# Soft-capped attention and MLP: the 64 left-over keys of two head pairs scored together, with longer tanh and exp and another order of transfers

## The chip, the cores and the metric

The kernel runs on one core of a Trainium2 chip. The metric is device time in microseconds of one execution; the time before is the median of three runs. All rows below come from one profiled execution of the kernel before.

## The reference

Attention with a tanh cap on the scores over 4 batches and 12 heads of 448 tokens and 64 dimensions, and behind it an MLP of 768 to 2048 to 768 with a squared ReLU on the 1792 tokens.

```python
scores = scale * np.matmul(q, k.transpose(0, 1, 3, 2))
scores = cap * np.tanh(scores / cap)
attn = np.exp(scores - np.max(scores, axis=-1, keepdims=True))
attn = attn / (np.sum(attn, axis=-1, keepdims=True) + 1e-09)
attn_out = np.matmul(attn, v)
x = attn_out.transpose(0, 2, 1, 3).reshape(B * S, H * D)
h = np.maximum(x @ w_in, 0.0)
out = h * h @ w_out
```

## The kernel before

Heads are taken two at a time: a "group" n is one pair of heads, 24 groups in all, and one round of the loop at line 498 works on group n and finishes group n - 1. One head of the pair lies in partitions 0 to 63 ("top"), the other in 64 to 127 ("bottom"). Scores are held with keys in the partitions and the 448 queries in the columns. The 448 keys of a head are three tiles of 128 (u = 1, 2, 3) and a rest of 64 (u = 0). A full tile of both heads fills two PSUM banks (128 x 896 on ScalarE); the rest of 64 keys of both heads fills one bank (128 x 448), the one head in its top half, the other in its bottom half.

The order on TensorE, ScalarE, VectorE, GpSimd and SyncE is the order in which the code is written (a manual schedule). A round does, with the names that the rows use:

- TensorE: `scores` of u = 1, 2, 3, then of u = 0 (`sc`); for group n - 1 `pv_half` (the 64 rest keys times v into `pa`, and times ones into `pb`), `sums` (`pb<-add,ones`) and `pv` (`pa<-p,vn`). Three score tiles of two banks each rotate, and one `pa` and one `pb`.
- ScalarE: tanh of u = 1 and 2, exp of both together (128 x 1792), tanh of u = 3 and u = 0, exp of both together (128 x 1344), and `evac`, the copy of `pa` of group n - 1 to SBUF (`e<-pa`). There are two `e` tiles, so the copy of group n - 1 needs the tile that `normalise` of group n - 3 reads.
- VectorE: `add_p3` of group n - 1 (`add<-add,p`), `turn_kq` of group n + 1 (a 32 x 32 transpose that makes q and k usable, `kq<-kqn`), `invert` of group n - 2 (`cmp`), a step of decoding MLP weights, `add_p` of group n (needs the first exp), `take_sums` (copy of `pb`, `es<-pb`), `normalise` of group n - 3 (`x<-e,rb` and two more), another decoding step. Some decoding steps (Abs, L44) are on ScalarE.
- SyncE issues the transfers, in this order: `spread` of group n - 3 (two transfers that read the inverted sums from DRAM into all partitions, `rb<-rd`), four loads of q for group n + 3, `rd<-cmp` of group n - 2 (inverted sums to DRAM) and `cmp<-es` of group n - 1 (two transfers). A transfer waits on the queue until what it reads is there, and what stands behind it waits too. `rb<-rd` waits for `rd<-cmp` of the round before to have landed.

So a group's row sums go from `es` through `cmp`, `rd` and `rb` back to VectorE, over two rounds. After the loop TensorE goes on with the first matrix product of the MLP; `unit(0, 0)` of it already stands in the last round, ahead of `pv_half` of the last group.

Of the kernel before, what the change touches and what calls it, by code (L numbers as in the profile page):

```python
# [10 lines left out]
F32 = mybir.dt.float32  # L11
# [4 lines left out]
ACTF = mybir.ActivationFunctionType  # L16
# [172 lines left out]
def tile_softcap_attention_mlp(ctx, tc, q, k, v, cap, w_in, w_out, out):  # L189
    nc = tc.nc  # L190
    B, H, S, D = q.shape
    NT, DM = out.shape
    DFF = w_in.shape[1]
    P = 128
# [8 lines left out]
    scale = 1.0 / float(D) ** 0.5  # L203
# [4 lines left out]
    NKV = 3  # L208
# [24 lines left out]
    qks = const.tile([P, 1], F32, name="qks")  # L233
# [4 lines left out]
    pp = actx.enter_context(tc.tile_pool(name="p", bufs=2))  # L238
    ep = actx.enter_context(tc.tile_pool(name="ep", bufs=2))
    ps_s = actx.enter_context(tc.tile_pool(name="ps_s", bufs=3, space=PSUM))  # L240
# [7 lines left out]
    vn = [keep.tile([P, NS, D], F32, name=f"vn{i}") for i in range(NKV)]  # L248

    ones = keep.tile([P, D], F32, name="ones")  # L250
# [63 lines left out]
    top, bottom = slice(0, D), slice(D, P)  # L314

    def load_kq(n, i, *queues):
        b, j = divmod(n, NPAIR)
        for a in range(4):
            h, w = divmod(a, 2)
            x = (k, q)[i][b, 2 * j + h, :, 32 * w:32 * w + 32].rearrange("(t r) e -> r t e", r=32)  # L320
            queues[a % len(queues)].dma_start(out=kqn[n % NKQ][32 * a:32 * a + 32, i], in_=x)  # L321

    def load_v(n):
        b, j = divmod(n, NPAIR)
        x, dst = v[b, 2 * j:2 * j + 2], vn[n % NKV]
        for h, r in enumerate((top, bottom)):
            nc.gpsimd.dma_start(out=dst[:, 3 * h:3 * h + 3], in_=x[h, 0:3 * P].rearrange("(u p) d -> p u d", u=3))  # L327
            nc.gpsimd.dma_start(out=dst[r, 6], in_=x[h, 3 * P:])

    NU = 4  # L330
    last = {}
# [2 lines left out]
    kqs, ps, probs, adds, pvs, es, rds = {}, {}, {}, {}, {}, {}, {}  # L334


    def turn_kq(n, parts=1):
        kqs[n] = qp.tile([P, 2 * S], F32, tag="kq", name="kq")
        src, w = kqn[n % NKQ].rearrange("p i t e -> p (i t e)"), 2 * S // parts
        for i in range(parts):  # L340
            done = nc.vector.transpose(out=kqs[n][:, i * w:(i + 1) * w], in_=src[:, i * w:(i + 1) * w])
            last.setdefault("turn", done)

    def scores(n, u):
        sc = ps_s.tile([P, 2, 512], F32, tag="s", name="sc")
        kt, qt = kqs[n][:, :S], kqs[n][:, S:]
        for h, r in enumerate((top, bottom)):
            if u:
                w = kt[r, (u - 1) * P:u * P]
                nc.tensor.matmul(out=sc[:, h, :S], lhsT=w, rhs=qt[r], start=True, stop=True)  # L350
            else:
                nc.tensor.matmul(out=sc[r, 0, :S], lhsT=kt[r, 3 * P:], rhs=qt[r], start=True, stop=True)  # L352
        probs[n, u] = sc

    def tanh(n, u):
        if u in (1, 3):
            c = 4 if u == 1 else 3
            t = pp.tile([P, c, S], F32, tag=f"p{c}", name="p")
            ps[n, u // 3] = t
        p = {1: slice(0, 2), 2: slice(2, 4), 3: slice(0, 2), 0: slice(2, 3)}[u]  # L360
        p = ps[n, int(u not in (1, 2))][:, p]
        nc.scalar.activation(out=p, in_=probs[n, u][:, :p.shape[1], :S], func=ACTF.Tanh, scale=qks)  # L362
        probs[n, u] = p

    def exp(n, i):
        p = ps.pop((n, i))
        nc.scalar.activation(out=p, in_=p, func=ACTF.Exp, scale=cap_sb)  # L367

    def add_p(n):
        adds[n] = pp.tile([P, 2, S], F32, tag="add", name="add")  # L370
        nc.vector.tensor_add(out=adds[n], in0=probs[n, 1], in1=probs[n, 2])  # L371

    def add_p3(n):
        nc.vector.tensor_add(out=adds[n], in0=adds[n], in1=probs[n, 3])


    def pv_half(n):
        pvs[n, 0] = ps_v.tile([P, S], F32, tag="pa", name="pa")
        pvs[n, 1] = ps_v.tile([P, S], F32, tag="pb", name="pb")
        p = probs.pop((n, 0))[:, 0]  # L380
        for h, (r, o) in enumerate(((top, bottom), (bottom, top))):
            nc.tensor.matmul(out=pvs[n, 0][r], lhsT=vn[n % NKV][r, 6], rhs=p[r], start=True, stop=False)  # L382
            nc.tensor.matmul(out=pvs[n, 1][o], lhsT=ones[r], rhs=p[r],
                             start=True, stop=False)


    def sums(n):
        a = adds.pop(n)
        for i in range(4):
            h, c = 1 - i // 2, slice(i % 2 * HS, (i % 2 + 1) * HS)  # L390
            nc.tensor.matmul(out=pvs[n, 1][32 * i:32 * i + 32, c], lhsT=ones[:, :32], rhs=a[:, h, c],  # L391
                             start=False, stop=True, tile_position=(0, 32 * i))
# [11 lines left out]


    def take_sums(n):
        e = ep.tile([P, S], F32, tag="es", name="es", bufs=NE)
        nc.vector.tensor_copy(out=e, in_=pvs.pop((n, 1)))
        rds[n] = ep.tile([P - 16, 8], F32, tag="cmp", name="cmp", bufs=NE)
        for c in range(2):  # L410
            nc.sync.dma_start(out=rds[n][c * 56:c * 56 + 56], in_=e[32 * c:P:64, c * HS:(c + 1) * HS])

    def invert(n):
        cmp = rds[n]
        nc.vector.tensor_scalar(out=cmp, in0=cmp, scalar1=guard[:P - 16], scalar2=None, op0=ALU.add)  # L415
        nc.vector.reciprocal(out=cmp, in_=cmp)
        rd = dram.tile([2, 2, HS], F32, tag="rd", name="rd")
        nc.sync.dma_start(out=rd.rearrange("c i (o e) -> (c i o) e", e=8), in_=cmp)
        rds[n] = rd


    def spread(n):
        rd = rds[n]
        rds[n] = ep.tile([P, S], F32, tag="rb", name="rb", bufs=2)
        for h, r in enumerate((top, bottom)):
            last["dma"] = nc.sync.dma_start(out=rds[n][r].rearrange("p (c q) -> p c q", c=2), in_=rd[:, 1 - h].partition_broadcast(D))  # L426

    def normalise(n):
        b, j = divmod(n, NPAIR)
        x = ep.tile([P, S], F32, tag="x", name="x", bufs=1)  # L430
        nc.vector.tensor_mul(out=x, in0=es.pop(n), in1=rds.pop(n))
        xs = xpool.tile([P, 2, S], F32R, tag="xs", name="xs")
        hi, lo = xs[:, 0], xs[:, 1]
        nc.vector.tensor_copy(out=hi, in_=x)
        last["dve"] = nc.vector.tensor_sub(out=lo, in0=x, in1=hi.bitcast(F32))
        xh[b, j], xl[b, j] = hi, lo
# [23 lines left out]
    def prepare_cap():  # L460

        nc.vector.tensor_scalar_mul(ncap, cap_sb, -1.0)
        nc.vector.tensor_tensor(out=ncap, in0=ncap, in1=cap_sb, op=ALU.min)
        nc.vector.tensor_scalar(out=far, in0=ncap[0:1], scalar1=-CAP_MAX, scalar2=None, op0=ALU.is_lt)

        nc.scalar.activation(out=guard, in_=ncap, func=ACTF.Exp)
# [20 lines left out]
    NE = 2  # L487
    AHEAD = 1, 0

    def decode(count):  # L490
        for _ in range(count):
            next(decoding, None)

    def unit(f, b):
        hps[b, f] = ps_s.tile([P, 2, 512], F32, tag="s", name="hps")[:, 0, :S]
        mlp1_part(b, f, 0, 3 * KDM)

    for n in range(NP + 1):
        on, prep, old = n < NP, n + 1 < NP, n > 0

        if on:
            for u in (1, 2, 3):
                scores(n, u)
            tanh(n, 1)
            tanh(n, 2)
            exp(n, 0)
            tanh(n, 3)
        if old:
            add_p3(n - 1)
        if n >= 3:  # L510
            spread(n - 3)
        if n + 3 < NP:
            load_kq(n + 3, 0, nc.gpsimd)
            load_kq(n + 3, 1, nc.sync)
        if prep:
            load_v(n + 1)
        if n == 0:
            prepare_cap()
        if prep:
            turn_kq(n + 1)  # L520
        if n == 1:
            nc.vector.tensor_scalar_mul(guard, guard, 1e-9)
        if n >= 2:
            invert(n - 2)
        decode(1)
        if on:
            scores(n, 0)
            tanh(n, 0)
            exp(n, 1)
        if n == NP:  # L530
            unit(0, 0)
        if old:
            pv_half(n - 1)
            sums(n - 1)
        if on:
            add_p(n)
        if old:
            take_sums(n - 1)
            pv(n - 1)
        if n >= 3:  # L540
            normalise(n - 3)
        if n:
            decode(1)
        if old:
            evac(n - 1)
# [120 lines left out]
    with ExitStack() as mctx:  # L666
# [128 lines left out]
        for z in range(-6, N + 1):  # L795
# [7 lines left out]
            if 0 <= z + 2 < N:  # L803
                m, i = PRODUCTS[z + 2]
                ops[m, i] = operand(raws[m, i])
            if 0 <= z < N:
                weights(z)
                m, i = PRODUCTS[z]
# [36 lines left out]
```

## Time and profile before

| what | us |
|---|---|
| median of 3 runs (632.57 to 636.3) | 635.08 |
| the profiled execution | 635.07 |
| its span, first to last instruction | 633.3 |
| PE busy (97% of the span) | 614.1 |
| DVE busy (74%) | 469.6 |
| ACT busy (54%) | 343.8 |
| mean granted TensorE clock, share of full speed | 0.994 |

The span is read as three stages: attention (about 8.6 to 184 us), the first MLP product (to about 421 us) and the second (to the end). The change lies in the first. Outside the span lie 1.8 us.

### The profile page before, as it was taken

Reading aid. Unit: us, or ns where it says so; the run is one execution under the profiler, and the core shown is the slowest. Engines: PE = TensorE matmul, PEld = TensorE weight load, DVE = VectorE, ACT = ScalarE, POOL = GpSimd, SP = SyncE. Lnnn points to the kernel's source line nnn. Section 1 sums busy time; section 2 is a strip of 40 time slices with the busy share of each in tenths; the row PEclk is TensorE's granted clock in tenths of the full one; section 3 lists DMA queues with packets and bytes.
Section 4 is the critical chain, followed back from the end, with each engine's and each line's share of the span. In section 5 each row is a group of like instructions: output and inputs, shape, how many; then the busy total and the mean of one; then the engine's idle time right before and its main releaser. Section 6 shows DMA issues by size and latency. Waiting matters only on the chain.

```text
span 633.3 us, 9649 instructions
## 1 busy us (share of the span) xinstructions
PE 614.1 (97%) x3412; PEld 485.4 (77%) x3412; DVE 469.6 (74%) x818; ACT 343.8 (54%) x444; POOL 123.9 (20%) x197
## 2 busy tenths in 40 slices
PE   6999898999999999999999999999999999999995
PEld 4333332333348998999999999999999999999994
DVE  3688787889877951489898999824799997666651
ACT  5999897999963322455565555535334642222210
POOL 8896676676300000000000000000000000000000
PEclk9999998999999999999999999999999999999998
DMA  9798677776424421566656877699499707555501
GB/s 150 146 140 157 119 144 130 151 129 150 93 56 147 149 98 59 175 219 195 185 195 205 248 255 231 219 250 344 129 279 289 196 14 211 150 155 162 161 37 43
DMA packets 157097, 103.94 MB, mean 164 GB/s; under 512 B 58896, under 2 KB 149392, under 8 KB 157040
## 3 DMA queue, kind: packets, MB, share of 16 engines
q1 hardware_dynamic: 148624, 92.05, 55.2%
q0 software_dynamic: 6880, 10.91, 7.7%
q8 instruction: 29, 0.48, 0.3%
q10 hardware_dynamic: 1536, 0.27, 0.3%
q14 instruction: 28, 0.23, 0.1%
HBM read 79.69 MB, written 23.42 MB: 163 GB/s over the span
## 4 chain that ended last, share of the span: by engine, by line
PE 75%; DMA 9%; ACT 7%; SPq 3%; DVE 2%; issue 2%; POOL 1%; DVEq 0%; ACTq 0%; POOLq 0%
PE hps L298 37%; PE po L692 32%; DMA rd<-cmp 5%; ACT p L362 3%; ACT p L367 3%; PE pa L398 2%; SPq L321 2%; DMA rb<-rd 2%; SPq L426 2%; PE sc L350 1%; DMA kqn<-in_k_dram 1%; DMA kqn<-in_q_dram 1%; PE pa L382 1%; PE sc L352 1%; PE pb L391 1%
## 5 line engine op out<-in xcount | busy, mean ns | idle before, releaser
L298 PE MATMUL hps<-xs,kq 128*128 128x448 f32 x864 | 175.1, 364 | 0.6 <-ACT r L302 0.6
L298 PEld LDWEIGHTS hps<-xs,kq 128*128 128x128 f32 x864 | 161.9, 187 | 13.7 <-ACT r L302 1.0
L692 PE MATMUL po<-th,gl 128*128 128x384 f32 x392 | 131.7, 336 | 0.0
L692 PE MATMUL po<-th,gh 128*128 128x384 f32 x392 | 131.6, 336 | 0.0
L692 PE MATMUL po<-tl,gh 128*128 128x384 f32 x392 | 131.6, 336 | 0.0
L681 ACT CAST gh<-a 128x1024 fp32r<-128x1024 f32 x49 | 51.5, 1052 | 111.7 <-PE po L692 101.0
L362 ACT ACTIVATE p<-sc,qks 128x896 f32<-128x896 f32 x96 | 82.5, 907 | 5.2 <-PE sc L350 5.2
L682 DVE TENSOR_TENSOR gl<-a,gh 128x1024 fp32r<-128x1024 f32 x49 | 59.9, 1223 | 32.4 <-ACT gh L681 32.4
L367 ACT ACTIVATE p<-p,cap_sb 128x1792 f32<-128x1792 f32 (+1 forms) x48 | 76.9, 1602 | 1.6
L692 PEld LDWEIGHTS po<-tl,gh 128*128 128x128 f32 x392 | 73.6, 188 | 0.0
L692 PEld LDWEIGHTS po<-th,gh 128*128 128x128 f32 x392 | 73.6, 188 | 0.0
L692 PEld LDWEIGHTS po<-th,gl 128*128 128x128 f32 x392 | 73.6, 188 | 0.0
L302 ACT ACTIVATE r<-hps 128x448 f32<-128x448 f32 x64 | 34.8, 544 | 68.8 <-PE hps L298 68.4
L321 POOL DMA_DIRECT2D kqn<-in_k_dram x92 | 58.6, 643 | 27.7 <-DVE cmp L415 20.0
L350 PE MATMUL sc<-kq 64*128 64x448 f32 x288 | 60.9, 554 | 3.0 <-DVE qks L457 1.7
L398 PE MATMUL pa<-p,vn 128*64 128x448 f32 x288 | 59.8, 551 | 0.0
L350 PEld LDWEIGHTS sc<-kq 64*128 64x128 f32 x288 | 25.8, 186 | 37.3 <-issue 19.6
L298 PE MATMUL hps<-xs,whi 128*128 128x448 f32 x192 | 54.1, 363 | 0.0
L398 PEld LDWEIGHTS pa<-p,vn 128*64 128x64 f32 x288 | 18.7, 137 | 31.5 <-issue 31.2
L327 POOL DMA_DIRECT2D vn<-in_v_dram x48 | 36.7, 764 | 18.9 <-PE pa L398 18.2
L298 PEld LDWEIGHTS hps<-xs,whi 128*128 128x128 f32 x192 | 35.8, 187 | 4.0 <-issue 1.4
L371 DVE TENSOR_TENSOR add<-p 128x896 f32<-128x896 f32 x24 | 26.2, 1092 | 13.7 <-ACT p L367 13.5
(80 smaller groups left out, 734.3 us busy)
## 6 DMA issues: line engine op xcount, KB each, us to landing
a<-g_dram SPq DMA_DIRECT2D x56, 512.0 KB
g_dram<-r SPq DMA_DIRECT2D x64, 224.0 KB
wraw<-in_moe_w_in_dram SPq DMA_DIRECT2D x32, 384.0 KB
wraw<-in_moe_w_out_dram SPq DMA_DIRECT2D x32, 384.0 KB
rb<-rd SPq DMA_DIRECT2D x48, 112.0 KB
kqn<-in_q_dram SPq DMA_DIRECT2D x93, 56.0 KB
out_dram<-osb SPq DMA_DIRECT2D x27, 192.0 KB
kqn<-in_k_dram POOLq DMA_DIRECT2D x92, 56.0 KB, 3.9
```

The source lines that it names most:

```text
L298: nc.tensor.matmul(out=ps, lhsT=w[:, c * P:(c + 1) * P], rhs=x[b, c], start=(n == 0), stop=(n == 3 * KDM - 1))
L302: nc.scalar.activation(out=r, in_=ps, func=ACTF.Relu)
L321: queues[a % len(queues)].dma_start(out=kqn[n % NKQ][32 * a:32 * a + 32, i], in_=x)
L327: nc.gpsimd.dma_start(out=dst[:, 3 * h:3 * h + 3], in_=x[h, 0:3 * P].rearrange("(u p) d -> p u d", u=3))
L350: nc.tensor.matmul(out=sc[:, h, :S], lhsT=w, rhs=qt[r], start=True, stop=True)
L362: nc.scalar.activation(out=p, in_=probs[n, u][:, :p.shape[1], :S], func=ACTF.Tanh, scale=qks)
L367: nc.scalar.activation(out=p, in_=p, func=ACTF.Exp, scale=cap_sb)
L371: nc.vector.tensor_add(out=adds[n], in0=probs[n, 1], in1=probs[n, 2])
L398: nc.tensor.matmul(out=pvs[n, 0][r], lhsT=vn[n % NKV][:, 3 * h + u - 1], rhs=p[:, h], start=False, stop=(u == NU - 1))
L681: nc.scalar.copy(out=hi, in_=x)
L682: nc.vector.tensor_sub(out=lo, in0=x, in1=f32(hi))
L692: nc.tensor.matmul(out=po, lhsT=w[:, c], rhs=m[:, cols], start=(c == 0 and i == 0), stop=(c == HF - 1 and i == 2))
```

## The change

The rest scores of an even group n and of the odd group n + 1 are computed together in round n, in one score tile of two banks (`half_scores`). For the odd group the heads change places in the tile (`rows`): the top head's scores go to the bottom partitions and the other way round, so that the four products use the four 64 x 64 quadrants of the array. One tanh takes both groups (128 x 896 in place of twice 128 x 448). In an even round the second exp then takes four slots (u = 3 of this group, and the rests of two groups: 128 x 1792), in an odd round two (128 x 896); before it was three slots in each. The rest of v of an odd group is loaded with the heads swapped, and `pv_half` takes the operands by `rows`, both products with v first and then both with ones. On VectorE `add_p3` moves behind `turn_kq`; `es` has one buffer; `normalise` works in place in `rb`. On SyncE the loads of q move ahead of `spread`.

```diff
+    def rows(n, h):
+        return bottom if (n + h) % 2 else top
...
-            if u:
-                w = kt[r, (u - 1) * P:u * P]
-                nc.tensor.matmul(out=sc[:, h, :S], lhsT=w, rhs=qt[r], start=True, stop=True)
-            else:
-                nc.tensor.matmul(out=sc[r, 0, :S], lhsT=kt[r, 3 * P:], rhs=qt[r], start=True, stop=True)
+            nc.tensor.matmul(out=sc[:, h, :S], lhsT=kt[r, (u - 1) * P:u * P], rhs=qt[r], start=True, stop=True)
         probs[n, u] = sc
+
+    def half_scores(n):
+        sc = ps_s.tile([P, 2, 512], F32, tag="s", name="sc")
+        for i in range(2):
+            kt, qt = kqs[n + i][:, :S], kqs[n + i][:, S:]
+            for h, r in enumerate((top, bottom)):
+                nc.tensor.matmul(out=sc[rows(n + i, h), i, :S], lhsT=kt[r, 3 * P:], rhs=qt[r], start=True, stop=True)
+        probs[n, 0] = sc
...
+            c = 2 if u == 3 and n % 2 else 4
+            ps[n, u // 3] = pp.tile([P, c, S], F32, tag=f"p{c}{u}", name="p", bufs=2 if c == 4 else 1)
+        at = 2 * (u in (2, 0))
+        p = ps[n, int(u not in (1, 2))][:, at:at + 2]
+        nc.scalar.activation(out=p, in_=probs[n, u][:, :, :S], func=ACTF.Tanh, scale=qks)
...
-        e = ep.tile([P, S], F32, tag="es", name="es", bufs=NE)
+        e = ep.tile([P, S], F32, tag="es", name="es", bufs=1)
...
-        x = ep.tile([P, S], F32, tag="x", name="x", bufs=1)
-        nc.vector.tensor_mul(out=x, in0=es.pop(n), in1=rds.pop(n))
+        x = rds.pop(n)
+        nc.vector.tensor_mul(out=x, in0=es.pop(n), in1=x)
...
-        if old:
-            add_p3(n - 1)
-        if n >= 3:
-            spread(n - 3)
         if n + 3 < NP:
             load_kq(n + 3, 0, nc.gpsimd)
             load_kq(n + 3, 1, nc.sync)
+        if n >= 3:
+            spread(n - 3)
...
             turn_kq(n + 1)
+        if old:
+            add_p3(n - 1)
...
+        if on and n % 2 == 0:
+            half_scores(n)
+            tanh(n, 0)
         if on:
-            scores(n, 0)
-            tanh(n, 0)
             exp(n, 1)
```

How the rows stand on SyncE in a middle round, first before:

```order
L418 DMA rd<-cmp 112x8
L411 DMA cmp<-es 56x1x8 x2
L426 DMA rb<-rd 64x2x224 x2
L321 DMA kqn_101<-in_q_dram 32x14x32 x4
L418 DMA rd<-cmp 112x8
```

And of the change, at the same place:

```order
L428 DMA rd<-cmp 112x8
L421 DMA cmp<-es 56x1x8 x2
L321 DMA kqn_101<-in_q_dram 32x14x32 x4
L436 DMA rb<-rd 64x2x224 x2
L428 DMA rd<-cmp 112x8
```

The four loads of q now stand between `cmp<-es` and the two `rb<-rd`, and no longer between `rb<-rd` and the next `rd<-cmp`.

On ScalarE two rounds of the change, an even one and then an odd one (before, every round is tanh x2, exp 128x1792, tanh 128x896, tanh 128x448, exp 128x1344, copy):

```order
L368 ACTIVATE p<-sc,qks 128x896 x2
L376 ACTIVATE p<-p,cap_sb 128x1792
L368 ACTIVATE p<-sc,qks 128x896 x2
L376 ACTIVATE p<-p,cap_sb 128x1792
L413 COPY e<-pa 128x448
L368 ACTIVATE p<-sc,qks 128x896 x2
L376 ACTIVATE p<-p,cap_sb 128x1792
L368 ACTIVATE p<-sc,qks 128x896
L376 ACTIVATE p<-p,cap_sb 128x896
L413 COPY e<-pa 128x448
```

The even round has grown by one half tanh and one slot of exp, the odd one has lost as much. On TensorE the same two rounds of the change:

```order
L351 MATMUL sc<-kq 128x448 x6
L359 MATMUL sc<-kq 64x448 x4
L392 MATMUL pa<-p,vn_104 64x448 x2
L395 MATMUL pb<-p,ones 64x448 x2
L401 MATMUL pb<-add,ones 32x224 x4
L408 MATMUL pa<-p,vn_104 64x448 x6
L351 MATMUL sc<-kq 128x448 x6
L392 MATMUL pa<-p,vn_105 64x448 x2
L395 MATMUL pb<-p,ones 64x448 x2
L401 MATMUL pb<-add,ones 32x224 x4
L408 MATMUL pa<-p,vn_105 64x448 x6
```

Before, two rest scores (64x448 x2) stood in each round; now four stand in the even one. They read q and k of the group after, so they need its transpose of the same round on VectorE.

## Rows read from the trace of the kernel before

**Rows 1.** Windows, attention stage: length; busy (count) of PE, PEld, DVE, ACT, POOL; clock, DMA, GB/s.

```profile
8.60:184.00 175.40, 167.28 (x1028) 59.19 (x1025) 141.21 (x241) 167.06 (x173) 116.46 (x182) 0.99 0.71 131
```

**Rows 2.** Timeline of ScalarE: start, length, engine, line, shapes; in brackets idle before.

```profile
22.53 1.91 ACT L362 ACTIVATE p<-sc,qks 128x896 f32<-128x896 f32 x2
...
66.70 0.53 ACT L403 COPY e<-pa 128x448 f32<-128x448 f32 x1 [2.08 <-DVE x L431]
...
158.43 1.79 ACT L367 ACTIVATE p<-p,cap_sb 128x1792 f32<-128x1792 f32 x1
160.13 1.51 ACT L362 ACTIVATE p<-sc,qks 128x896 f32<-128x896 f32 x2
161.68 1.42 ACT L367 ACTIVATE p<-p,cap_sb 128x1344 f32<-128x1344 f32 x1
163.00 0.51 ACT L403 COPY e<-pa 128x448 f32<-128x448 f32 x1
163.41 1.91 ACT L362 ACTIVATE p<-sc,qks 128x896 f32<-128x896 f32 x2
165.35 1.79 ACT L367 ACTIVATE p<-p,cap_sb 128x1792 f32<-128x1792 f32 x1
...
170.33 1.91 ACT L362 ACTIVATE p<-sc,qks 128x896 f32<-128x896 f32 x2
```

**Rows 3.** ScalarE's waits to 200 us: total, times, longest; then its decoding steps' group.

```profile
ACT e L403 <- DVE x L431: 5.6, 5, 2.1
...
L44 ACT ACTIVATE mag<-wraw 128x384 f32<-128x384 f32 x6 | 3.3, 548 | 0.0
```

**Rows 4.** Timeline of TensorE, a late round and the end of attention.

```profile
164.59 0.59 PE L352 MATMUL sc<-kq 64*64 64x448 f32 x2
...
166.24 0.59 PE L391 MATMUL pb<-add,ones 128*32 128x224 f32 x8
...
169.16 2.53 PE L350 MATMUL sc<-kq 64*128 64x448 f32 x12
...
183.22 0.68 PE L298 MATMUL hps<-xs,whi 128*128 128x448 f32 x2
...
187.02 0.59 PE L382 MATMUL pa<-p,vn 64*64 64x448 f32 x1
...
187.93 0.58 PE L391 MATMUL pb<-add,ones 128*32 128x224 f32 x8
```

**Rows 5.** Timeline of VectorE in the same round.

```profile
160.25 1.09 DVE L371 TENSOR_TENSOR add<-p 128x896 f32<-128x896 f32 x1 [0.24 <-ACT p L367]
161.26 0.62 DVE L408 COPY es<-pb 128x448 f32<-128x448 f32 x1
161.80 0.62 DVE L431 TENSOR_TENSOR x<-e,rb 128x448 f32<-128x448 f32 x1
...
163.89 1.08 DVE L374 TENSOR_TENSOR add<-add,p 128x896 f32<-128x896 f32 x1
```

**Rows 6.** Timeline of SyncE's queue: start and time taken by issuing, transfers.

```profile
60.41 1.31 SPq L426 DMA_DIRECT2D rb<-rd  x2
...
77.27 2.16 SPq L321 DMA_DIRECT2D kqn<-in_q_dram  x4
79.54 0.42 SPq L418 DMA_DIRECT2D rd<-cmp  x1
80.01 1.16 SPq L411 DMA_DIRECT2D cmp<-es  x2
83.12 1.29 SPq L426 DMA_DIRECT2D rb<-rd  x2
```

**Rows 7.** Timeline of VectorE: three waits for a transfer.

```profile
17.20 1.11 DVE L341 STREAM_TRANSPOSE kq<-kqn 128x896 f32<-128x896 f32 x1 [0.80 <-DMA kqn<-in_q_dram]
...
65.99 0.63 DVE L431 TENSOR_TENSOR x<-e,rb 128x448 f32<-128x448 f32 x1 [2.57 <-DMA rb<-rd]
...
86.99 0.63 DVE L431 TENSOR_TENSOR x<-e,rb 128x448 f32<-128x448 f32 x1 [0.34 <-DMA rb<-rd]
```

More of the change, by code (lines that the diff above doesn't have):

```diff
@@ L325, in load_v @@
         x, dst = v[b, 2 * j:2 * j + 2], vn[n % NKV]
-        for h, r in enumerate((top, bottom)):
+        for h in range(2):
             nc.gpsimd.dma_start(out=dst[:, 3 * h:3 * h + 3], in_=x[h, 0:3 * P].rearrange("(u p) d -> p u d", u=3))
-            nc.gpsimd.dma_start(out=dst[r, 6], in_=x[h, 3 * P:])
+            nc.gpsimd.dma_start(out=dst[rows(n, h), 6], in_=x[h, 3 * P:])
     NU = 4
@@ L347, in scores @@
         for h, r in enumerate((top, bottom)):
-            if u:
-                w = kt[r, (u - 1) * P:u * P]
-                nc.tensor.matmul(out=sc[:, h, :S], lhsT=w, rhs=qt[r], start=True, stop=True)
-            else:
-                nc.tensor.matmul(out=sc[r, 0, :S], lhsT=kt[r, 3 * P:], rhs=qt[r], start=True, stop=True)
-        probs[n, u] = sc
+            nc.tensor.matmul(out=sc[:, h, :S], lhsT=kt[r, (u - 1) * P:u * P], rhs=qt[r], start=True, stop=True)
+        probs[n, u] = sc
+    def half_scores(n):
[5 more added lines that the diff above has]
+        probs[n, 0] = sc
     def tanh(n, u):
         if u in (1, 3):
[L357 to L363, printed above, removed]
+            c = 2 if u == 3 and n % 2 else 4
[3 more added lines that the diff above has]
+        nc.scalar.activation(out=p, in_=probs[n, u][:, :, :S], func=ACTF.Tanh, scale=qks)
+        if u:
+            probs[n, u] = p
+        else:
+            probs[n, 0], probs[n + 1, 0] = p[:, 0], p[:, 1]
     def exp(n, i):
@@ L379, in pv_half @@
         pvs[n, 1] = ps_v.tile([P, S], F32, tag="pb", name="pb")
[L380 to L384, printed above, removed]
+        p = probs.pop((n, 0))
+        for h, o in enumerate((top, bottom)):
+            r = rows(n, h)
+            nc.tensor.matmul(out=pvs[n, 0][o], lhsT=vn[n % NKV][r, 6], rhs=p[r], start=True, stop=False)
+        for h, o in enumerate((bottom, top)):
+            r = rows(n, h)
+            nc.tensor.matmul(out=pvs[n, 1][o], lhsT=ones[r], rhs=p[r], start=True, stop=False)
     def sums(n):
```

## The prediction

> **What bounds the kernel now.** I read the windows by stage first. In the attention stage ScalarE is busy 167.06 of 175.40 us, TensorE 167.28, VectorE 141.21 [rows 1]: two engines are nearly full, and a gain on one alone may be worth nothing. So I went to ScalarE's timeline. A round takes 6.92 us from one first exp to the next (158.43 to 165.35), with no idle time in it [rows 2]; ScalarE sets the pace there. From the tanh of group 2 (22.53) to that of group 22 (170.33) 20 rounds take 147.80 us, where 20 x 6.92 = 138.4. Of the 9.4 us over, four decoding steps (four of the six of rows 3 lie in this stretch) take 4 x 0.45 = 1.8: 548 ns less 0.10, by which neighbours on this engine overlap (161.68 + 1.42 = 163.10 against 163.00). The other 7.6 us are waits: the copy of `pa` waited five times, 5.6 us, for `normalise` on VectorE to free its tile [rows 3], and the rest is what those waits break behind them. VectorE in turn waited for `rb<-rd` [rows 7]. So what bounds attention is ScalarE's own work, and at times the way of the row sums through SyncE's queue.
>
> TensorE comes next. It is last only at the very end of the loop.
>
> **What the change does to ScalarE.** All times here are in the frame of rows 2 and 5: a first exp ends at 158.43 + 1.79 = 160.22, the tanh of u = 3 starts at 160.13, and from the start of the copy to the end of the next first exp 4.14 us pass (163.00 to 165.35 + 1.79). Two full tanh and the exp behind them: 1.94 (163.41 to 165.35). A full tanh alone: 1.00, since two take 1.91 with 0.10 overlap. An exp slot is worth (1.79 - 1.42) = 0.37, so the exp of two slots, which no row has, takes 1.42 - 0.37 = 1.05 by the slope of the other two.
> - Even round: exp starts at 160.13 + 1.94 = 162.07, the copy can start at 162.07 + 1.79 - 0.10 = 163.76, the next first exp ends at 167.90. Length 7.68.
> - Odd round: exp at 160.13 + 1.00 + 0.03 = 161.16, the copy could start at 161.16 + 1.05 - 0.10 = 162.11. Length 6.03 if it does.
>
> The pair would be 13.71 against 13.84: one tanh's fixed part is saved, less the overlap that the odd round loses. But in the odd round the copy is now ready too early. `normalise` reads its tile from 161.80 to 162.42, and this instant hangs on the first exp (`add_p` at 160.25, `take_sums` at 161.26, then x) [rows 5], which the change leaves where it was. The copy follows 0.08 behind (66.70 against 65.99 + 0.63) [rows 2, 7], at 162.50. The odd round is 162.50 + 4.14 - 160.22 = 6.42, the pair 14.10: **0.26 slower** than two rounds now.
>
> **TensorE.** A rest by itself, four 64 x 64 products in two passes, takes 0.91 (187.02 to 187.93, `pv_half` of the last group); now the rest scores and `pv_half` of a round take 1.65 together (164.59 to 166.24) [rows 4]. A pair has 3 x 0.91 = 2.73 in place of 3.30, so 0.57 is saved; TensorE drops to about 13.5 a pair, under ScalarE's 14.10, so this is worth nothing on the path. What it costs is a new wait: the four rest scores need the transpose of the next group. It moves ahead of `add_p3`, to 163.89, and ends at 165.00 after 1.11 [rows 5, 7]. Then 0.91, 0.91, `sums` and `pv` 2.92 (166.24 to 169.16) and a third of the scores, 2.53 / 3 = 0.84 [rows 4], end at 170.58. The tanh that waits for them wants to start at 162.50 + 0.41 + 7.68 = 170.59. So there is no slack; for two handovers I count **0.10 a pair**. Were the transpose still behind `add_p3`, it would be 1.0 more. `add_p3` itself ends about 1.1 later, at 166.1, still before `sums` wants it (166.8).
>
> **SyncE's order.** Let E be the end of the `es` copy. Now: `cmp<-es` (1.16), `rb<-rd` as soon as the old `rd` has landed, q, and `rd` behind q. An `rd` issued right behind q landed at 83.12, 3.69 after q's issue had ended (77.27 + 2.16), though it is tiny [rows 6]. After: `cmp<-es`, q (2.16), then `rb<-rd` (1.29): with gaps of 0.05 the second `rb<-rd` is out at E + 4.75. The late `rd`s are cured, since `rd` now has a full round to land. But every `rb` stands behind q. From the end of its issue to x it takes between 2.58 (83.12 + 1.29 to 86.99) and 4.27 (60.41 + 1.31 to 65.99) [rows 6, 7], so it is there at E + L with L between 7.33 and 9.02. From x to the next E: 0.62 + 0.08 + 4.14 + 1.66 = 6.50 (the last is 161.26 + 0.62 - 160.22). x of a round is not before L behind the E of the round before, so two rounds take at least L + 6.50. This decides from L = 7.7 on (14.20 - 6.50). I take 7.85: something tiny behind q would land at E + 3.4 + 3.69 = E + 7.1, the rest is `rb`'s own data; it is 3.1 behind the issue, nearer to the low end. That is 14.35 a pair, 0.15 more than 14.20, in the nine pairs that still load q: 1.4. Late landings like the one at 60.41 (1.69 over 2.58) I count twice: 3.4. Together **4.8**, with bounds 0 (L = 7.33) and 9 x 1.32 = 12 (L = 9.02).
>
> The Trainium skill speaks to this point: "DMA: Bandwidth & Descriptors", Queues, rings and completion order, has it that on each transfer engine the descriptors of one issuing engine are consumed in ring order. By that rule `rb` waits out all of q's data whatever its size; the 3.69 us of the tiny `rd` agree. By the rule alone nothing below L = 7.1 could be had, and the sum would keep its value.
>
> **Start and end.** In the first pair `add_p3` now stands behind the transpose that waits for q until 17.20 [rows 7]. It ends at 17.20 + 1.11 + 1.09 - 0.10 = 19.3; `sums` and `pv` 2.92 and a first score tile with handover 0.94 follow, and the tanh of group 2 starts at 23.2 in place of 22.53: **+0.7**. At the end, TensorE starts the MLP at 183.22, 12.89 after the tanh of group 22 [rows 2, 4]. After: the transpose ends 2.09 behind that tanh, then 0.91 + 0.91 + 2.92 + 2.46 + 0.91 + 2.92, 13.1: **+0.2**. From there on TensorE works without a break in both kernels, so this shift goes to the end whole.
>
> **At nothing:** one `es` buffer (`invert`, ahead of the next copy on VectorE, waits for the same transfers already), x in place of `rb` (two buffers, refilled two rounds on), the order in `pv_half` and the swapped rest of v (same transfers, same products). The cover is a TensorE with 0.6 us spare a pair; gone, the order in `pv_half` could cost 0.91 at most.
>
> **The sum**, over the ten pairs from group 2 to 22: 10 x (0.26 + 0.10) = +3.6; queue +4.8; start +0.7; end +0.2; waits of now gone -7.6. Total +1.7 on the profiled execution's 635.07, which stands at the median of 635.08: **636.8 us**. Half a percent, 3.2 us, is about what a measurement of this kernel can tell from no change.
>
> **The rivals.**
> - *The queue binds (slower).* If q's data hold `rb` up to L = 8.5 as a rule, nine pairs take 15.0 and the queue costs 9 x 0.8 + 3.4 = 10.6: 635.07 + 3.6 + 10.6 + 0.9 - 7.6 = 642.6. For it: 4.27 was seen, and k is loaded at the same time; against it: 2.58. It decides from L = 7.7. Chance 0.23.
> - *The waits go and none comes (faster).* With L at 7.3 and no late landing the queue costs 0: 632.0; if also the copy in the odd round finds x done and TensorE is in time, the pair is 13.71 and ten pairs gain 1.3: 635.07 - 1.3 + 0.9 - 7.6 = 627.1. For it: five waits are all that ScalarE has now; against it: x starts at a fixed distance from the first exp. Chance 0.28.
> - *The four rest scores don't run side by side (slower).* They would take 1.82 and the next tanh start 0.9 later in each of 12 pairs: about 647. Against it: at 187.02 four quadrants did, two of them into the bank of `pa` [rows 4]. The Trainium skill ("TensorEngine Tiling (Array Packing)", PSUM Pressure) says that different row tiles cannot access the same PSUM bank at once; rest scores do that too, and the trace of `pv_half`, 0.91 for all four, goes against it. Chance 0.06.
> - *No change that shows:* 633 to 638.2, the forecast. Chance 0.43.
>
> The remaining faster and slower cases reach 629.5 below and 643.5 above, with about one in ten left out on each side. Faster by over 0.5%: 0.28; within: 0.43; slower: 0.29.
>
> **What would show it.** Right: pairs of rounds of about 7.7 and 6.4 us by the first exps; the odd copies waiting 0.3 to 0.4 for VectorE; exp of two slots at 1.05; four rest scores in about 0.9; `rb<-rd` no more waiting for `rd`, and x waiting for `rb` in even rounds. Wrong: TensorE idle ahead of a first score tile, so that tanh waits; `rb` landing well under E + 7.3, or a pair at 13.7.

## The result, and the profile after

The changed kernel takes 643.06 us (median of 4 runs, 642.66 to 644.41) against 635.69 for the kernel before beside it (4 runs): ratio 1.0126, 95% interval 1.0083 to 1.0168. It is slower by 1.3%, where no change that shows was forecast; the time lies just inside the range, at the rival "the queue binds". The profiled execution took 643.34 us, span 641.6, 8.3 us more than the one before.

All of it is lost in attention. TensorE's first MLP product starts at 192.64 (row 192.64 below) instead of 183.22 [rows 4], 9.4 us later; from there to the end the changed kernel is 1.15 us shorter (643.34 - 192.64 = 450.7 against 635.07 - 183.22 = 451.85). The windows of attention, with the columns of [rows 1]; then four short stretches of the same view, each behind a stop of TensorE:

```profile
8.60:193.50 184.90, 168.70 (x1028) 58.45 (x1025) 140.70 (x240) 166.78 (x162) 117.20 (x182) 0.97 0.62 125
...
19.70:24.00 4.30, 4.30 (x18) 1.31 (x16) 3.82 (x5) 2.12 (x3) 3.69 (x6) 0.60 0.81 188
...
52.40:57.00 4.60, 4.60 (x28) 1.81 (x24) 4.53 (x8) 3.92 (x6) 3.11 (x5) 1.00 0.30 73
...
68.10:72.70 4.60, 4.53 (x22) 1.39 (x24) 4.05 (x10) 3.17 (x3) 1.88 (x3) 0.65 0.25 55
...
136.30:141.00 4.70, 4.70 (x28) 1.58 (x30) 4.00 (x7) 4.63 (x5) 2.53 (x4) 0.65 0.39 101
```

ScalarE is busy 166.78 of 184.90 us: the same work as before in a stretch 9.5 us longer. So waits have come in, not work. In three of the short stretches TensorE's granted clock is 0.60 or 0.65 of its full 2.4 GHz, near the lower level of 1.2 GHz; in the one from 52.40 it is 1.00.

ScalarE's timeline at three places: the start of group 2, a pair in the middle that goes wrong, and a late pair that doesn't (in brackets the idle time before, and what ended it):

```profile
24.01 0.53 ACT L413 COPY e<-pa 128x448 f32<-128x448 f32 x1 [2.19 <-PE pa L408]
24.94 1.91 ACT L368 ACTIVATE p<-sc,qks 128x896 f32<-128x896 f32 x2 [0.40 <-PE sc L351]
...
55.84 1.91 ACT L368 ACTIVATE p<-sc,qks 128x896 f32<-128x896 f32 x2 [0.40 <-PE sc L351]
...
65.17 0.53 ACT L413 COPY e<-pa 128x448 f32<-128x448 f32 x1 [2.00 <-DVE rb L441]
65.60 1.91 ACT L368 ACTIVATE p<-sc,qks 128x896 f32<-128x896 f32 x2
...
72.71 0.53 ACT L413 COPY e<-pa 128x448 f32<-128x448 f32 x1 [1.41 <-PE pa L408]
73.63 1.91 ACT L368 ACTIVATE p<-sc,qks 128x896 f32<-128x896 f32 x2 [0.39 <-PE sc L351]
...
165.47 1.91 ACT L368 ACTIVATE p<-sc,qks 128x896 f32<-128x896 f32 x2
...
173.22 1.90 ACT L368 ACTIVATE p<-sc,qks 128x896 f32<-128x896 f32 x2
...
177.87 1.04 ACT L376 ACTIVATE p<-p,cap_sb 128x896 f32<-128x896 f32 x1
179.22 0.53 ACT L413 COPY e<-pa 128x448 f32<-128x448 f32 x1 [0.31 <-DVE rb L441]
179.65 1.91 ACT L368 ACTIVATE p<-sc,qks 128x896 f32<-128x896 f32 x2
```

The late pair is as forecast: 165.47 to 173.22 is 7.75 us, 173.22 to 179.65 is 6.43, together 14.18 (forecast 14.20); the exp of two slots takes 1.04 (1.05), and the odd copy waits 0.31 for VectorE. At 65.17 the copy waits 2.00 us for VectorE's product with `rb`, and a round later it waits again, now for TensorE, 1.41 us, and the tanh behind it 0.39. That second wait is the one the prediction didn't have. ScalarE's waits over the 20 rounds, 24.9 to 179.6 us (total, times, longest); then, from 24 to 182 us, those of x (VectorE's product with `rb`) for `rb`, and those of TensorE's matmuls for `add_p3`:

```profile
ACT e L413 <- DVE rb L441: 9.0, 8, 2.9
ACT e L413 <- PE pa L408: 2.6, 4, 1.4
ACT p L368 <- PE sc L351: 2.0, 5, 0.4
```

```profile
DVE rb L441 <- DMA rb<-rd: 13.5, 10, 2.9
...
PE pb L401 <- DVE add L383: 6.1, 5, 2.2
```

The waits on VectorE were 5.6 us before [rows 3] and are now 9.0, and behind them stand 2.6 us for `pv` and 2.0 for the first score tile. TensorE in turn waits 6.1 us for `add_p3`, which is not among the matmuls' waits before at all in this stretch; each of these five waits follows an x that waited for `rb`. TensorE's timeline at the start, around 52 us and in the middle pair:

```profile
19.25 0.59 PE L401 MATMUL pb<-add,ones 128*32 128x224 f32 x8 [2.27 <-DVE guard L532]
19.77 4.17 PE L408 MATMUL pa<-p,vn 128*64 128x448 f32 x12
...
26.32 0.98 PE L359 MATMUL sc<-kq 64*64 64x448 f32 x8
27.12 0.54 PE L395 MATMUL pb<-p,ones 64*64 64x448 f32 x2
...
51.85 0.59 PE L401 MATMUL pb<-add,ones 128*32 128x224 f32 x8 [2.21 <-DVE add L383]
52.36 2.48 PE L408 MATMUL pa<-p,vn 128*64 128x448 f32 x12
...
68.17 0.97 PE L401 MATMUL pb<-add,ones 128*32 128x224 f32 x8 [1.43 <-DVE add L383]
69.08 3.56 PE L408 MATMUL pa<-p,vn 128*64 128x448 f32 x12
...
192.64 0.67 PE L298 MATMUL hps<-xs,whi 128*128 128x448 f32 x2
```

At 19.25 and 68.17 TensorE has waited for VectorE; the `pv` behind takes 4.17 and 3.56 us in place of 2.48, at the lowered clock. At 51.85 it has waited as long, 2.21 us, and the clock stays at 1.00 and `pv` at 2.48. The four rest scores take 0.80 (26.32 to 27.12). VectorE at the same places:

```profile
17.11 1.11 DVE L344 STREAM_TRANSPOSE kq<-kqn 128x896 f32<-128x896 f32 x1 [3.75 <-DMA kqn<-in_q_dram]
18.15 1.05 DVE L383 TENSOR_TENSOR add<-add,p 128x896 f32<-128x896 f32 x1
...
60.61 0.62 DVE L418 COPY es<-pb 128x448 f32<-128x448 f32 x1
64.14 0.62 DVE L441 TENSOR_TENSOR rb<-e,rb 128x448 f32<-128x448 f32 x1 [2.92 <-DMA rb<-rd]
...
66.04 1.10 DVE L344 STREAM_TRANSPOSE kq<-kqn 128x896 f32<-128x896 f32 x1
67.07 1.05 DVE L383 TENSOR_TENSOR add<-add,p 128x896 f32<-128x896 f32 x1
...
124.18 0.62 DVE L441 TENSOR_TENSOR rb<-e,rb 128x448 f32<-128x448 f32 x1 [0.74 <-DMA rb<-rd]
```

Here is the chain of the middle pair: x waits 2.92 us for `rb` and starts at 64.14, 3.53 after the `es` copy of 60.61 began; the transpose follows at 66.04, `add_p3` at 67.07, and at its end, 68.12, TensorE's `sums` can begin. The pair from the tanh of 55.84 to that of 73.63 (ScalarE's rows) takes 17.79, 3.6 more than an undisturbed one. And SyncE's queue ahead of that x, with a usual `rb<-rd` below it:

```profile
55.87 0.39 SPq L263 DMA_DIRECT2D wraw<-in_moe_w_in_dram  x1
56.31 2.13 SPq L321 DMA_DIRECT2D kqn<-in_q_dram  x4
58.49 1.31 SPq L436 DMA_DIRECT2D rb<-rd  x2
...
119.64 1.32 SPq L436 DMA_DIRECT2D rb<-rd  x2
```

At 55.87 a load of MLP weights (`wraw`) stands ahead of q, and both ahead of `rb<-rd`: x starts 4.34 us after the end of the issue (58.49 + 1.31 to 64.14); in the usual case of 119.64 it is 3.22 (to 124.18). `wraw` can't be all of it: at 41.43 `rb<-rd` stands behind q alone, and x starts 4.62 us after the end of its issue.

### The profile page after: what moved, and what is told of

The parts are those of the page before. It is cut to its first block, busy times and chain, and to the rows that moved or that the text cites. A ratio compares the mean times of both kernels' runs of the same rounds, so it can differ in the third digit from the quotient of the medians.

```text
span 641.6 us, 9620 instructions
## 1 busy us (share of the span) xinstructions
PE 616.7 (96%) x3412; PEld 485.8 (76%) x3412; DVE 469.8 (73%) x818; ACT 343.5 (54%) x432; POOL 124.7 (19%) x197
## 4 chain that ended last, share of the span: by engine, by line
PE 79%; DMA 6%; ACT 5%; DVE 5%; SPq 3%; issue 1%; POOL 1%; DVEq 0%; ACTq 0%; POOLq 0%
PE hps L298 36%; PE po L703 32%; PE pa L408 5%; DMA rb<-rd 4%; ACT p L368 2%; PE sc L351 2%; ACT p L376 2%; SPq L321 1%; PE pb L401 1%; PE sc L359 1%; DVE add L380 1%; DMA kqn<-in_k_dram 1%; PE pa L392 1%; DVE kq L344 1%; SPq L421 1%
## 5 line engine op out<-in xcount | busy, mean ns | idle before, releaser
L368 ACT ACTIVATE p<-sc,qks 128x896 f32<-128x896 f32 x84 | 80.4, 1000 | 6.7 <-PE sc L351 6.7
L408 PE MATMUL pa<-p,vn 128*64 128x448 f32 x288 | 62.2, 569 | 0.0
```

Of the source, the lines that this page charges most:

```text
L368: nc.scalar.activation(out=p, in_=probs[n, u][:, :, :S], func=ACTF.Tanh, scale=qks)
L408: nc.tensor.matmul(out=pvs[n, 0][r], lhsT=vn[n % NKV][:, 3 * h + u - 1], rhs=p[:, h], start=False, stop=(u == NU - 1))
```

## The experiments

The theory: the loss comes from `rb` standing behind q on SyncE's queue, by way of x. The rivals: it comes from `add_p3` standing behind the transpose, at the start and after; or from the pairing itself, the rounds of unequal length and the four rest scores.

In all of these the ratio is to the kernel before on the same chip, whose median was 635.2, 634.7 and 634.2 us in the three sets.

**Four cells of two orders.** The changed kernel has two reorderings beside the pairing. The first three runs undo one, the other, or both.

*e1*, the order of SyncE put back:

```diff
+        if n >= 3:
+            spread(n - 3)
         if n + 3 < NP:
             load_kq(n + 3, 0, nc.gpsimd)
             load_kq(n + 3, 1, nc.sync)
-        if n >= 3:
-            spread(n - 3)
```

> The change with one thing undone: on SyncE rb<-rd stands ahead of the loads of q again. Theory A (q ahead of rb makes x late, and that costs most of the 8 us): x no longer waits over 2 us, the 20 rounds from group 2 to 22 fall from 154.7 us to about 148 to 150 (14.2 a pair plus the late rd of the kernel before), time 636 to 639. Theory B (VectorE's order, sums of TensorE waiting for add_p3 behind the transpose, costs it by itself): within 1.5 us of the change's 643.

Measured: 634.69 us, ratio 0.9993 (0.9967 to 1.0018). The whole loss is gone, and the time is below even theory A's 636 to 639: 20 rounds from group 2 take 146.2 us (154.7 in the changed kernel, 147.8 before), though group 2 still starts late, at 24.61.

*e2*, the order of VectorE put back:

```diff
-        if prep:
-            turn_kq(n + 1)
         if old:
             add_p3(n - 1)
+        if prep:
+            turn_kq(n + 1)
```

> The change with add_p3 ahead of the transpose on VectorE again. Theory A: the rest scores of the next group wait 1 us longer in every pair and the score tile behind them with them, so 643 to 650, not faster; the start alone gains up to 2 us. Theory B: TensorE's sums wait no more, 637 to 640.

Measured: 642.59 us, ratio 1.0124 (1.0090 to 1.0158). The start is cured (tanh of group 2 at 22.04), but 20 rounds take 156.2: what is won there is lost again in the rounds, since the rest scores now wait 9.9 us for the transpose.

*e3*, both put back, so that the pairing, the longer tanh and exp and the order in `pv_half` are left:

```diff
+        if n >= 3:
+            spread(n - 3)
         if n + 3 < NP:
...
-        if n >= 3:
-            spread(n - 3)
...
-        if prep:
-            turn_kq(n + 1)
         if old:
             add_p3(n - 1)
+        if prep:
+            turn_kq(n + 1)
```

> Both orders undone, only the pairing of the rest scores, the longer tanh and exp and the order in pv_half are left. Theory A: between the first experiment and the change, 638 to 645, since the transpose is late for the rest scores. Theory B: the fastest of the three, under 637.

Measured: 638.14 us, ratio 1.0067 (1.0043 to 1.0091). x waits only 0.2 us for `rb` from 24 to 182 us, but the even rounds behind the first take 8.4 to 8.95 us; TensorE's waits of that stretch:

```profile
PE sc L359 <- DVE kq L344: 9.5, 10, 1.1
```

That is the 1.0 us a pair which the prediction gave for a transpose that stays behind `add_p3`. So of the two reorderings the one on VectorE gains for the pairing (e3 against e1: 3.4 us net of what it costs at the start), and the one on SyncE costs 8.4 us (e1 against the changed kernel). The two don't simply add: with `add_p3` first the order on SyncE costs 4.5 us (e2 against e3), and with q first the order on VectorE is worth nothing (e2 against the changed kernel).

**The queue order by itself.** *e4*, the kernel before with q ahead of `rb`:

```diff
-        if n >= 3:
-            spread(n - 3)
         if n + 3 < NP:
             load_kq(n + 3, 0, nc.gpsimd)
             load_kq(n + 3, 1, nc.sync)
+        if n >= 3:
+            spread(n - 3)
```

> The kernel before with only the order on SyncE changed: q ahead of rb<-rd. Theory A: x waits for rb as in the change, 638 to 643. A third theory, C (the new order of the queue is good or neutral, since it cures the late rd, and the pairing loses the time): 632 to 636.

Measured: 636.76 us, ratio 1.0033 (1.0008 to 1.0057): a loss of some 2 us, between the two theories, and a quarter of what the same order costs in the changed kernel. x waits for `rb` 13.0 us, as much as there (13.5 in the same stretch), and the copy 6.7 us for x; but the waits of TensorE's matmuls are one line, and none is for `add_p3`:

```profile
PE sc L352 <- ACT p L362: 7.4, 9, 2.2
```

The same lateness costs less here. What differs in the traces is that TensorE's matmuls never wait here for what stands behind x. That this is the reason is argued, not shown: the pairing by itself already raises the price from 2 to the 4.5 us of e2 against e3, and the kernel before with both orders changed was not run.

**The next set** tries the queue further, and the start.

*e5*, the q load on SyncE behind `rd` too:

```diff
-        if n + 3 < NP:
-            load_kq(n + 3, 0, nc.gpsimd)
-            load_kq(n + 3, 1, nc.sync)
         if n >= 3:
             spread(n - 3)
+        if n + 3 < NP:
+            load_kq(n + 3, 0, nc.gpsimd)
...
             invert(n - 2)
+        if n + 3 < NP:
+            load_kq(n + 3, 1, nc.sync)
```

> The changed kernel with both copies of rb's fetch ahead of the q load (as in e1), and the q load now behind the copy of the reciprocals to DRAM (rd) on SyncE's queue, so that neither rd nor rb stands behind a q load of the same round. Theory A (what costs is the stretch from the end of the copy of es to the landing of rb, L; anything of small pieces that stands ahead of one of its three transfers lengthens it): L falls below the 7.7 us at which a round of an undisturbed pair begins to wait, x waits on rb under 6 us in all (11.6 us in e1, 13.9 in the changed kernel), time 632 to 634 us (e1 634.7). Rival A2 (the q load only meets the next transfers of the sums instead, the copy of es into cmp): L stays at 7.6 to 8.2, x waits 10 to 13 us, time 634 to 636.

Measured: 633.06 us, ratio 0.9973 (0.9952 to 0.9994). x waits 0.4 us for `rb` from 24 to 182 us (9.2 in e1), and 20 rounds take 143.2. Ten undisturbed pairs of 14.18 and the decoding are 143.6: with `rb` in time, and x in its old place on VectorE, nothing of the loss is left in the rounds. SyncE's queue, one round:

```profile
70.35 0.33 SPq L428 DMA_DIRECT2D rd<-cmp  x1
70.72 1.99 SPq L321 DMA_DIRECT2D kqn<-in_q_dram  x4
72.75 1.16 SPq L421 DMA_DIRECT2D cmp<-es  x2
74.01 1.29 SPq L436 DMA_DIRECT2D rb<-rd  x2
```

`rd`, then q, then `cmp` and `rb`: q no longer stands between `cmp` and `rb`. What it can hold up now is `cmp`, and `invert` waits 3.8 us for that (0.9 in the changed kernel).

*e9*, e5 with `add_p3` of group 0 ahead of the transpose in that one round, and *e10*, the changed kernel with that alone:

```diff
+        if n == 1:
+            add_p3(0)
         if prep:
             turn_kq(n + 1)
-        if old:
+        if n > 1:
             add_p3(n - 1)
```

> e5 with the second half of the sum of slots (add_p3) of group 0 ahead of the transpose of group 2, and the transpose first in all other rounds. Theory: the start and the steady part are separate terms. The tanh of group 2 starts at 21.9 to 22.2 us (24.6 in e1, 22.04 in e2), pv of group 0 runs at 2.4 GHz, and time is 2.0 to 3.0 us below e5, 629.5 to 632. Rival (the gain at the start is taken back by waits for the loads of q, k and rb, which do not start earlier by as much): within 0.8 us of e5.

> The changed kernel with only the order of that one round put back (add_p3 of group 0 ahead of the transpose of group 2). It sizes the start's term by itself: tanh of group 2 at 21.9 to 22.2 us (24.94 in the changed kernel), and 640.0 to 641.5 us (643.06) if the start is added to what follows; within 0.8 us of 643 if the rounds behind it take it back.

Measured: e9 629.92 us, 0.9922 (0.9894 to 0.9950), 3.1 less than e5; e10 639.63 us, 1.0076 (1.0048 to 1.0104), 0.5% or some 3 us less than the changed kernel. Tanh of group 2 starts at 22.07 and 22.14. TensorE at the start of e10:

```profile
17.13 0.58 PE L401 MATMUL pb<-add,ones 128*32 128x224 f32 x8
17.64 2.48 PE L408 MATMUL pa<-p,vn 128*64 128x448 f32 x12
```

`sums` no longer waits and `pv` takes its 2.48. The start is a term of its own, some 3 us.

*e11*, the kernel before with the transpose first:

```diff
-        if old:
-            add_p3(n - 1)
...
         if prep:
             turn_kq(n + 1)
+        if old:
+            add_p3(n - 1)
```

> The kernel before with the transpose of the next group ahead of add_p3 on VectorE in all rounds, and nothing else. Together with e3, e1 and the changed kernel it tells whether the 3.4 us that this order is worth in the changed kernel (e3 638.1, e1 634.7) come from the pairing: there the rest scores of the next group stand in the same round and wait for its transpose. Theory: in the kernel before nothing in a round needs the next transpose so early, so that only the start is lost: 636 to 638 us, tanh of group 2 near 24.6. Rival (the earlier transpose is a gain by itself): 632 to 634.

Measured: 633.73 us, ratio 0.9993 (0.9970 to 1.0017). The time is that of the rival, but the kernel before stood at 634.7 in this set, so there is no gain; nor is there the loss at the start: tanh of group 2 moved by 0.5 us only, to 23.02. TensorE stood 1.13 us for `add_p3` there, the granted clock stayed at 1.00, and `pv` took 2.48.

**What is late behind x.** *e12*, three `e` buffers (paid for with one relu tile less in the MLP), so that the copy waits for no x, and *e13*, which also moves x behind the transpose and `add_p3` of the next round. Both keep q ahead of `rb`.

```diff
-    tmp = rctx.enter_context(tc.tile_pool(name="tmp", bufs=3))
+    tmp = rctx.enter_context(tc.tile_pool(name="tmp", bufs=2))
...
-        es[n] = ep.tile([P, S], F32, tag="e", name="e", bufs=NE)
+        es[n] = ep.tile([P, S], F32, tag="e", name="e", bufs=3)
```

e13 adds to it:

```diff
             add_p3(n - 1)
+        if n >= 4:
+            normalise(n - 4)
...
-        if n >= 3:
+        if n == NP:
             normalise(n - 3)
```

> The changed kernel with three buffers instead of two for the copy of pa (e), paid for by one buffer less (of three) of the relu tiles that only the matmuls behind the attention use. The copy then no longer waits for the x of two groups earlier; x stands where it stood on VectorE, ahead of the transpose and add_p3 of the next round. Theory D (a late rb costs through the copy that waits for x): the 20 rounds from group 2 to 22 fall from 154.7 us to 146 to 149, and the time to 634 to 638. Theory K (it costs through the transpose and add_p3 that stand behind x on VectorE, for which the sums and pv wait): the rounds stay at 152 to 156 us and the time at 640 to 645.

> e12 with x of a group moved on VectorE from the end of its round to behind the transpose and add_p3 of the next round, so that a late rb holds up neither of them nor, by the third buffer, the copy. The queue order is that of the changed kernel (q ahead of rb). Theory (a late rb is the whole cause beyond the start): no waits of the sums for add_p3 that begin at an rb, 20 rounds in 143 to 147 us, time 632 to 636. Rival (the late q load or PE's own order is part of the cause): 149 us or more, 638 or more.

Measured: e12 643.98 us, ratio 1.0173 (1.0144 to 1.0201); its profiled execution was the shortest, 639.31, with 151.1 us for the 20 rounds and group 2 already at 22.56. Undisturbed rounds are now 7.65 and 6.02 long, since the odd copy waits for no x; ten such pairs and the decoding would take 138.5, so 12.6 us of waits are left. ScalarE's waits from 24 to 182 us, then those of TensorE's matmuls:

```profile
ACT e L413 <- PE pa L408: 6.2, 4, 4.3
ACT p L368 <- PE sc L351: 4.4, 13, 0.4
```

```profile
PE pb L401 <- DVE add L383: 4.6, 4, 3.4
PE sc L359 <- DVE kq L344: 4.3, 5, 1.2
```

No copy waits for x any more, and by the median nothing is won: it waits for `pv` instead, which waits for `sums`, `add_p3` and the transpose. e13: 627.39 us, ratio 0.9903 (0.9880 to 0.9926), by the two ratios 2.2% under the changed kernel, with the queue's order unchanged, and below the 632 to 636 expected. (The MLP, with one relu tile less, takes no less than before: 627.43 - 175.21 = 452.2 from its first product, against 451.85 and the changed kernel's 450.7.) Two of its rounds, and the windows view of the 20:

```profile
149.59 1.91 ACT L368 ACTIVATE p<-sc,qks 128x896 f32<-128x896 f32 x2
...
157.25 1.91 ACT L368 ACTIVATE p<-sc,qks 128x896 f32<-128x896 f32 x2
...
161.91 1.04 ACT L376 ACTIVATE p<-p,cap_sb 128x896 f32<-128x896 f32 x1
162.86 0.51 ACT L413 COPY e<-pa 128x448 f32<-128x448 f32 x1
163.27 1.91 ACT L368 ACTIVATE p<-sc,qks 128x896 f32<-128x896 f32 x2
```

```profile
24.87:163.27 138.40, 134.72 (x886) 47.69 (x884) 120.25 (x206) 137.12 (x135) 101.27 (x158) 1.00 0.69 141
```

149.59 to 157.25 and on to 163.27 is 7.66 and 6.02, a pair of 13.68; the 20 rounds take 138.40, which is ten of these and the decoding (138.6) and not one wait more. The start of group 2 is as late as in the changed kernel (24.87). Of the 16.3 us between these 20 rounds and the changed kernel's 154.7, 5.0 are the odd copy's wait for an x that is in time (ten times 14.18 - 13.68), which the third buffer took away; the other 11.3 came from a late `rb`, and e5 gives the same, 11.5, by the queue alone. A late `rb` has two ways to ScalarE, the copy, and the transpose and `add_p3` that stand behind x on VectorE; the second is enough to keep the time where it was (e12), and with both gone no wait is left. The second taken away by itself, with two `e` buffers, was not tried.

**Is it the pairing that gains?** *e6*, the kernel before with q behind `rd` (the move of e5), and *e14*, the kernel before with the orders of e9:

```diff
             load_kq(n + 3, 0, nc.gpsimd)
-            load_kq(n + 3, 1, nc.sync)
...
             invert(n - 2)
+        if n + 3 < NP:
+            load_kq(n + 3, 1, nc.sync)
```

> The kernel before with the q load moved behind the copy of rd on SyncE's queue (rb's fetch ahead of it, as it was), and nothing else. It tells whether e5's place of the q load is a gain without the pairing too. If the waits on rb and cmp are all that stands above the 6.92 us of an undisturbed round, 20 rounds fall from 147.8 us to 139 to 143 and the time to 627 to 631 us. Rival: another wait shows instead in rounds of 6.9 us, which leave a transfer less time than pairs of 14.1 us; 632 to 635.

> The kernel before with the orders of e9 (transpose ahead of add_p3 but in the round of group 1, q load behind rd), without the pairing and the longer tanh and exp. Beside e9 (629.9) it tells what the pairing is worth where no transfer is late. Theory by undisturbed rounds (two of 7.03 us here by e11, 14.1 in a pair of e9): the same within 2 us, 628 to 632. Rival (two rounds of 7 us leave rb and cmp less time than a pair of 7.7 and 6.4): 632 to 635.

Measured: e6 627.36 us, ratio 0.9903 (0.9881 to 0.9925), 20 rounds in 140.5; e14 628.80 us, 0.9920 (0.9897 to 0.9943). e14 and e9 (0.9922) differ by the pairing, with its longer tanh and exp, and the small terms that the prediction put at nothing: together nothing that can be told here. The best without pairing (e6) and the best with it (e13) are equal. That doesn't settle which is better: e13 with the start of e10 or the queue of e6 was not tried, nor the kernel before with e13's third buffer and later x.

## Why the prediction was wrong

Of the forecast's terms, in the profiled execution:

| term | forecast | measured |
|---|---|---|
| pairs, 10 x (0.26 + 0.10) | +3.6 | an undisturbed pair 14.18: +3.4 |
| queue | +4.8 | 154.71 - 142.0 - 1.8 = +10.9 |
| start | +0.7 | 24.94 - 22.53 = +2.4 |
| end | +0.2 | 12.99 against 12.89: +0.1 |
| waits of now | -7.6 | taken out in the queue's term |

(154.71 is the time from the tanh of group 2 to that of group 22, 24.94 to 179.65; 142.0 is ten forecast pairs, 1.8 the decoding. By ten measured pairs, 141.8, the queue's term is 11.1, and the terms add up to the 9.4 us by which the MLP starts later; the MLP itself took 1.15 less, which the forecast had at nothing.)

**The queue term was the step that failed**: the place was right, its size was 10.9 in place of 4.8, and one of the two ways of a late x to ScalarE was left out. Its usual L of 7.85 held: of the ten x that waited for `rb` in the 20 rounds, seven show an L (end of the `es` copy to x) of 7.6 to 8.4. But three landings were late, not two, and by more than 1.69: L was 9.39, 10.01 and 10.66. The last two stand behind q and a `wraw` load, which the prediction's list of the queue left out. By the step's own formula, L + 6.50 - 14.20 each, the ten add up to 8.8 at most. The rest, 2 us or more, is what the formula has no place for. It let a late x hold up the copy alone, once; it holds up the transpose and `add_p3` too, then `sums` and `pv`, then the copy and the tanh of the next round. The sentence "`add_p3` itself ends about 1.1 later, at 166.1, still before `sums` wants it (166.8)" is true only of a round whose x is in time. In the 20 rounds ScalarE waited 9.0 us for x, of which some 0.31 in each odd round was forecast, and by this second way 4.6 us for TensorE, which was not. e12 shows that the second way by itself is enough to keep the time (take the copy's wait away, and nothing is won), e13 that with both ways gone no wait is left, e4 that in the kernel before, where `add_p3` stands first, a late `rb` reaches ScalarE by the copy almost alone and costs 2 us.

**The start** failed in its last step: `add_p3` was forecast to end at 19.3 and did at 19.20, but `sums` and `pv` were taken at the 2.92 us of a busy TensorE. It had stood idle for 2.27 us, the granted clock in the 4.3 us that follow was 0.60, and `pv` took 4.17 in place of 2.48: the missing 1.7 us. e10 confirms the term's size. The clock's part of it does not come each time: in e12's profiled execution, with the same order, the transpose began 0.7 us earlier, TensorE stood 1.76 us, the clock stayed at 1.00, `pv` took 2.48, and group 2 began at 22.56.

**What held:** the undisturbed pair, the waiting odd copy, the exp of two slots, the price of a transpose that comes late (e3), the end. The rival "not side by side" is refuted by rest scores of 0.80. The rule of the Trainium skill that was weighed against it ("TensorEngine Tiling (Array Packing)", PSUM Pressure: different row tiles cannot use one PSUM bank at once) does not show as time here, though quadrants of both row halves write one bank. The rival "the waits go and none comes" was right in its arithmetic, 13.71 for a pair whose copy finds its tile free (13.68 in e13), but not for this kernel. The rival "the queue binds" gave 642.6 by L = 8.5 as a rule; the time fits, the way does not: the usual L stayed at 7.9, and few late ones, carried on, cost as much. That x waits 13.5 us for an `rb` behind q (changed kernel) and 0.4 for one with q out of its way (e5) agrees with the ring order of the Trainium skill ("DMA: Bandwidth & Descriptors", Queues, rings and completion order).

Open: what makes the late ones late. In the five runs with q ahead of `rb` and x in its place (the changed kernel, e2, e4, e10, e12), an awaited `rb` behind `wraw` and q was used 3.9 to 5.3 us after the end of its issue, ten times of ten; the other awaited ones mostly under 3.8, but up to 5.0. The round of 41.43, with an L of 9.39 and no `wraw` ahead, shows over 4 us in four of these five runs. Transfers of GpSimd's queue run at the same time; no run took them away, or `wraw`.

## What to carry to other kernels

Price a late transfer by everything that stands behind the waiting instruction on its in-order engine, and ask of each item when its own reader wants it; taking one of two ways out may show nothing (e12). Move the work that waits behind the work that others wait for (e13, with a third buffer: 2.2% under the changed kernel), or put the bulky load on the queue where the transfers behind it are not the ones wanted next (e6: 1% under the kernel before): neither changes the work itself. A change of the work itself is best judged where no transfer is late: with its own queue order this one costs 1.3%, between e14 and e9 nothing can be told.

## What was not expected of the hardware

An idle time of TensorE can cost twice: the wait, and a lowered clock behind it. After the stop of 2.27 us that ended at 19.25 the granted clock was 0.60 over 4.3 us, in which `pv` took 1.7 us longer. After two stops of 1.4 us, ended at 65.76 and 68.17, it was 0.65 over 4.6 us, and `pv` took 1.1 longer; after one of 2.76 us, ended at 136.30, it was 0.65 over 4.7 us.

It need not: the stop of 2.21 us that ended at 51.85 left the clock at 1.00. Other runs show both too. In the kernel before a stop of 1.94 us (ended at 98.73) was followed by 0.60 over 4.3 us, one of 1.91 (ended at 68.20) by 1.00; at the start, 2.00 us in e1 were followed by 0.60, 1.76 in e12 by 1.00. The length of one stop does not tell which it will be, and no run here shows what does. e13, whose matmuls wait for no `add_p3`, has 1.00 through its 20 rounds. So a stall's second price has to be read from the window behind it, stall by stall.
